# A third raw buffer and a second scaled buffer for the first block's weight tiles, in the space of the norm's tiles

## The chip, the cores and the metric

The kernel runs on one core of one Trainium2 chip. The metric is the device time of one execution in microseconds (us). TensorE (PE), VectorE (DVE), ScalarE (ACT) and GpSimd (POOL) each work through a list of instructions of their own, in order. SyncE (SP) issues all data transfers (DMAs) from one list, also in order: a transfer whose data or whose target is not ready holds back all that stand behind it.

## The reference

A linear attention with a decaying state gives 3072 rows of 384 values, and two feed-forward blocks follow.

```python
def _attn_ref(r, k, v, w, u):                 # (4, 8, 768, 48): batch, heads, steps, head size
    for t in range(S):
        kt, vt, rt, wt = (k[:, :, t], v[:, :, t], r[:, :, t], w[:, :, t])
        cur = np.einsum('bhd,bhe->bhde', u[None] * kt, vt)
        y[:, :, t] = np.einsum('bhd,bhde->bhe', rt, state + cur)
        state = wt[:, :, :, None] * state + np.einsum('bhd,bhe->bhde', kt, vt)
...
def _moe_ref(x, w_in, w_out):                 # 384 -> 2048 -> 384
    h = x @ w_in
    relu6 = np.clip(h + 3.0, 0.0, 6.0)
    g = h * relu6 / 6.0
    return g @ w_out
...
def _moe2_ref(x, w_gate, w_val, w_out, rms_g):   # 384 -> 1536 -> 384
    rms = np.sqrt(np.mean(x * x, axis=-1, keepdims=True) + 1e-06)
    xn = x / rms * rms_g
    g = xn @ w_gate
    silu = g * (1.0 / (1.0 + np.exp(-g)))
    val = xn @ w_val
    return silu * val @ w_out
```

The weights arrive as 64-bit floats, and the chip computes in 32 bits, so every weight tile is converted on the chip.

## The kernel before

**Chunks and steps.** The tokens are cut into six chunks of 512 columns (4 batches of 128 time steps). The first feed-forward block goes over the chunks c = 0 to 5 and, in each, over 16 weight tiles f = 0 to 15, one step per tile. In chunk 0, called the first block here, tiles 0 to 4 are done for the first 256 columns (steps n = 0 to 4) and then for the second 256 (n = 5 to 9), and tiles 5 to 15 for all 512 (n = 10 to 20). Chunk 1 begins at n = 21, also in half steps (n = 21 to 28 and 29 to 36). After chunk 5 follows the second feed-forward block.

A step does a first product on PE (`hps`, L353 in chunk 0, L347 later), the activation in two instructions (ACT L364, DVE L365), and the second product (`o`, L359 in chunk 0, L376 later) two steps later: `todo` holds two second products back. In chunk 0 the matmuls are plain 32-bit ones. Each `hps` has one of two PSUM buffers, which L365 frees.

**Weights.** `Weight.load` (L132) fetches a raw tile of 128 x 768 64-bit values (786 KB). `scale` (ACT, L140) brings its high words to the right exponent in a tile `mag`. `bits` (DVE, L145, L146, L148) puts the 32-bit number together in `x` from the raw tile and `mag`, and sends it to its place `wpair` by a transfer (SP, L153). `parts` (ACT L159, DVE L160) splits the tile in two for the later chunks, eleven steps after its first use (f + 11). Tile f is converted in a step n given by `begun`: f = 2 to 6 in n = 0 to 4, f = 7 and 8 in n = 7 and 8, f = 9 to 15 in n = 10 to 16. `load(f + 2)` stands in the same step right behind `bits(f)`.

**Attention.** One job per chunk and batch. The four jobs of chunk 1 (jobs 4 to 7) run beside the steps of chunk 0: job 4 begins at n = 11, job 5 at n = 15, job 6 at n = 19. From a job's step n: scans (DVE L182) and bonus (POOL L209, L210) at n; products and a sum (DVE L205, L214) at n + 1; `fill` (ACT L240, 8 instructions), `pe_a` (PE L259), `pe_kt` (PE L247) and `choose` (DVE L265, 2 instructions) at n + 2; `pe_y` (PE L295, L301), `pe_u` (PE L274), `copy_y` (ACT L307) at n + 3. `pe_y` writes the PSUM buffer that `choose` reads, and uses what `choose` wrote. For the jobs 0 to 3 of chunk 0, `pe_kt`, `copy_kt`, `pe_u` and `add_u` (ACT L281) lie in n = 2 to 6; `pe_kt` and `pe_u` share one PSUM buffer, so each `pe_kt` waits for the `add_u` before it. The loads for job 4 (`w`, `rk`, `rks`, `v`: 128 x 1040, 1024, 768 and 512 32-bit values) stand at the end of n = 7, those for job 5 (`w`, `rk`, `v`) at the end of n = 9.

**Order.** Three lists per step, `before`, `between` and `behind`, hold what runs ahead of the first product, between it and the second product, and behind it. `pin` then fixes the order of each engine as the program is written. A pool hands out buffers in rotation: a tile with `bufs=2` waits until the last reader of the tile before the previous one is done.

```python
    begun = {f: f - 2 for f in range(2, W1)} | {7: 7, 8: 8} | {f: f + 1 for f in range(9, F1)}
    for f, n in begun.items():
        before[n] += [wa[f].scale]
        behind[n] += [wa[f].bits]
        if f + 2 < F1:
            behind[n] += [wa[f + 2].load]
```

Of the kernel before, what the change touches and what calls it, by code (L numbers as in the profile page):

```python
# [9 lines left out]
F32 = mybir.dt.float32  # L10
F32R = mybir.dt.float32r
U32 = mybir.dt.uint32
U64 = mybir.dt.uint64
# [9 lines left out]
DM = H * D  # L23
KT = DM // 128
F1 = 2048 // 128
# [11 lines left out]
def kernel(  # L37
# [17 lines left out]
    def pool(stack, name, bufs=1, **kw):  # L55
        return stack.enter_context(tc.tile_pool(name=name, bufs=bufs, **kw))
# [9 lines left out]
    wp = pool(ctx, "wp", side="left")  # L66
    xt_p = pool(ctx, "xt", 2, side="left")
    rg_p = pool(ctx, "rg", 3, side="left")
    nm_p = pool(ctx, "nm", side="left")
    actx = ctx.enter_context(ExitStack())  # L70
    at_p = pool(actx, "at", 2, side="left")
    a1_p = pool(actx, "a1", side="left")
# [1 line left out]
    st_p = pool(tctx, "st", 2, side="left")  # L74
# [32 lines left out]
    def pin():  # L107
        fresh = []
        for x in reversed(nc.cur_bb.bb.instructions):
            if x.name in pinned:  # L110
                break
            fresh.append(x)
        for x in reversed(fresh):
            pinned.add(x.name)
            if x.engine in ENGINES:
                if x.engine in newest:
                    tc.add_manual_dep(x, newest[x.engine], NOSYNC, reason="program order")
                newest[x.engine] = x.name
# [2 lines left out]

    mag_bufs = 1

    class Weight:
        def __init__(self, src, dst, pairs):
            self.src, self.dst, self.pairs, self.near = src, dst, pairs, False

        def load(self):  # L130
            self.raw = st_p.tile([128, 2 * DM], U64, tag="raw", name="raw", bufs=2)
            nc.sync.dma_start(out=self.raw, in_=self.src.rearrange("p a n -> p (a n)"))  # L132

        def words(self):
# [1 line left out]
            return bits[:, :, 0], bits[:, :, 1]  # L136

        def scale(self):
            self.mag = st_p.tile([128, 2 * DM], F32, tag="mag", name="mag", bufs=mag_bufs)
            nc.scalar.activation(out=self.mag, in_=self.words()[1].bitcast(F32), func=AF.Copy, scale=2.0 ** -112)  # L140

        def bits(self):
# [288 lines left out]
    wa = [Weight(wa_d[f], None, False) for f in range(F1)]  # L431
# [8 lines left out]
    before, between, behind = ([[] for _ in steps] for _ in range(3))  # L440
# [16 lines left out]
    j0, j1, j2, j3 = jobs[:B]  # L457
# [17 lines left out]

    begun = {f: f - 2 for f in range(2, W1)} | {7: 7, 8: 8} | {f: f + 1 for f in range(9, F1)}
    for f, n in begun.items():
        before[n] += [wa[f].scale]
        behind[n] += [wa[f].bits]
        if f + 2 < F1:  # L480
            behind[n] += [wa[f + 2].load]
    for f in range(F1):
        before[f + 11] += [wa[f].parts]
    behind[7] += [lambda: jobs[4].load("w", "rk", "rks", "v")]
# [14 lines left out]
    def ff1(c, f, cols):  # L499
        n = cols.stop - cols.start  # L500
        ps = ps_h.tile([128, n], F32, tag="h", name="hps")
        if c == 0:
            if cols.start:
                wa[f].x = wpair[f][:, :, 1, :].bitcast(F32)
            emit_h_f32(wa[f].x[:, 0], xts[c][:, :, :, cols], ps)
            g = rg_p.tile([128, n], F32, tag="g", name="g")
            emit_act(ps, n, g)
        else:
            emit_h(wpair[f][:, 0], xts[c][:, :, :, cols], ps)
            a = rg_p.tile([128, n], F32, tag="a", name="a", bufs=2)  # L510
            emit_act(ps, n, a)
            g = emit_split(a, n)
        x = wa[f].x[:, 1] if c == 0 else wpair[f][:, 1]
        todo.append(lambda: ff2(c, f, cols, g, x))
# [13 lines left out]
    def run(fs):  # L528
        for x in fs:
            x()  # L530

    def load_x(c):
        x = xt_p.tile([128, KT, 2, TOK], F32R, tag="xt", name="xt")
        raw = b_p.tile([128, KT, TOK], F32, tag="xraw", name="xraw", bufs=1)
        nc.sync.dma_start(out=raw, in_=xn_d[c])
        xns[c] = x

        def part(k):
            nc.scalar.activation(out=x[:, k, 0, :], in_=raw[:, k, :], func=AF.Copy)
            nc.vector.tensor_tensor(  # L540
                out=x[:, k, 1, :], in0=raw[:, k, :], in1=x[:, k, 0, :].bitcast(F32), op=ALU.subtract)
        return part
# [22 lines left out]
    nc.sync.dma_start(out=ub, in_=u_d.to_broadcast([128, DM]))  # L565
    nc.sync.dma_start(out=gain, in_=g_d)
    wa[2].load()
    wa[3].load()
    nc.vector.memset(dd, 0.0)
    nc.vector.memset(half, 0.5)  # L570
    nc.vector.memset(eps, 1e-6)
# [4 lines left out]
        wa[f].dst = wpair[f]  # L576
        wa[f].near = f < 2
    run((j0.scans, j0.pairs, j0.pe_bonus, j0.muls, j0.fill, j0.pe_a, j1.scans, j1.pairs, j1.pe_bonus, j1.muls))
    run((j0.choose, j1.fill, j1.pe_a, j0.pe_y0, wa[0].scale, wa[0].bits, j1.choose, j1.pe_y0))
    run((j0.copy_y0, wa[1].scale, wa[1].bits, j1.copy_y0, j2.scans))  # L580
    pin()


    for n, (c, f, cols) in enumerate(steps):
        if n == W1:
            sctx.close()
            wp2 = pool(ctx, "wp2", side="right", reuse_waits="tile")
            wpair += [wp2.tile([128, 2, 2, DM], F32R, name=f"wpair{i}") for i in range(W1, F1)]
            for i in range(W1, F1):
                wa[i].dst = wpair[i]  # L590
        if n == first[1]:
            tctx.close()
        if n == first[NC_ - 1]:
            actx.close()
            st_p = pool(ctx, "st2", 2, side="left", reuse_waits="tile")
            mag_bufs = 2
            b_p = pool(ctx, "bp", 2, side="left", reuse_waits="tile")
            bw_p = pool(ctx, "bw", side="left", reuse_waits="tile")
            begun2 = {f: f * NE // F1 for f in range(F1) if (f + 1) * NE // F1 > f * NE // F1}
            extra += [bw_p.tile([128, 2, 2, DM], F32R, name=f"bpair{i}") for i in range(NX)]  # L600
            wb = [Weight(wb_d[i], extra[i] if i < NX else wpair[i - NX], True) for i in range(NB)]
            wb[0].load()
            wb[1].load()
        run(before[n])
        if c == NC_ - 1:
            if f == 4:
                part = load_x(0)
            if 8 <= f < 8 + KT:
                part(f - 8)

            if f - 2 in begun2:
                wb[begun2[f - 2]].parts()
        ff1(c, f, cols)
        run(between[n])
        while len(todo) > 2:
            todo.pop(0)()
        if c == NC_ - 1 and f in begun2:
            wb[begun2[f]].scale()
        run(behind[n])
        if c == NC_ - 1 and f in begun2:  # L620
            wb[begun2[f]].bits()
            wb[begun2[f] + 2].load()
        pin()
# [145 lines left out]
```

## Time and profile before

| | |
|---|---|
| median of 3 runs | 1025.42 us (1025.32 to 1026.27) |
| profiled execution, own time | 1027.49 us |
| its span in the trace | 1025.7 us |
| PE, DVE, ACT, POOL busy | 982.3, 484.3, 393.9, 346.4 us |
| mean granted TensorE clock | 0.987 of full |
| first step of chunk 1 (first L347) begins | 147.42 us |

Busy time is what an engine's instructions took; the span runs from the first instruction of the trace to the last. The execution's own time holds 1.8 us more than the span. The granted clock is the share of TensorE's full clock that the chip gave; it has two levels, half (1.2 GHz) and full (2.4 GHz). In the views below, a bracket at the end of a row is idle time of that engine ahead of the instruction, and what ended it.

### The profile page before, as it was taken

To read this page: it belongs to the slowest core of one execution; us is meant where nothing else is said; L and a number is where in the kernel's file an instruction comes from. 1 tells how busy PE (TensorE), PEld (TensorE's weight loads), DVE (VectorE), ACT (ScalarE), POOL (GpSimd) and SP (SyncE) were. 2 spreads that over 40 slices of the span, in tenths; PEclk is the share of its full clock that TensorE was granted. 3 is DMA by queue.
4 is the path that set the end of the run, shared out by engine and by line. 5 is a ranking of instruction groups with operands and counts; after the bars stand their busy time and mean duration, and the time that the engine had idled before them with its cause. 6 is when DMAs were issued, how large, how long until landed. Compare 5 with 4: busy or idle time off the path is not lost.

```text
span 1025.7 us, 13752 instructions
## 1 busy us (share of the span) xinstructions
PE 982.3 (96%) x5385; PEld 782.4 (76%) x5385; DVE 484.3 (47%) x627; ACT 393.9 (38%) x753; POOL 346.4 (34%) x306
## 2 busy tenths in 40 slices
PE   5797998889999999999999999999999999999998
PEld 4674457877888888787787788888888888888886
DVE  7848756665457646665389996112112112112111
ACT  3433535544544454455356554222222222222212
POOL 0002214545465574565353352222222222222221
PEclk9899989999999999999999999999999999999999
DMA  8557522333322332231242450200100100100000
GB/s 320 173 202 276 183 90 81 123 130 102 122 76 79 120 134 75 109 92 64 100 144 103 156 182 1 93 1 1 62 1 1 61 1 1 62 1 1 31 1 31
DMA packets 36768, 91.92 MB, mean 90 GB/s; under 512 B 5984, under 2 KB 17120, under 8 KB 36704
## 3 DMA queue, kind: packets, MB, share of 16 engines
q1 hardware_dynamic: 36704, 91.05, 25.6%
q8 instruction: 42, 0.69, 0.3%
q14 instruction: 22, 0.18, 0.0%
HBM read 71.37 MB, written 9.44 MB: 79 GB/s over the span
## 4 chain that ended last, share of the span: by engine, by line
PE 79%; DVE 9%; ACT 4%; DMA 4%; issue 3%; SPq 1%; POOL 0%; ACTq 0%; DVEq 0%; POOLq 0%
PE o L376 27%; PE gps L347 14%; PE vps L347 14%; PE hps L347 12%; DMA raw<-in_dram 3%; PE aps L259 2%; PE yps L301 2%; DVE x L146 2%; PE o L359 2%; PE yps L295 1%; DVE x L148 1%; PE hps L353 1%; DVE a L365 1%; PE ktp L247 1%; DVE w L182 1%
## 5 line engine op out<-in xcount | busy, mean ns | idle before, releaser
L376 PE MATMUL o<-g,wpair 128*128 128x512 f32 (+1 forms) x1287 | 306.1, 382 | 0.0
L376 PEld LDWEIGHTS o<-g,wpair 128*128 128x128 f32 x1287 | 230.4, 189 | 48.8 <-issue 0.7
L370 POOL TENSOR_TENSOR g<-s,g 128x512 fp32r<-128x512 f32 x72 | 96.8, 1344 | 338.4 <-ACT g L369 338.4
L663 DVE TENSOR_TENSOR s<-s,vps 128x512 f32<-128x512 f32 x72 | 49.5, 687 | 301.3 <-PE vps L347 300.4
L347 PE MATMUL hps<-xt,wpair 128*128 128x512 f32 (+1 forms) x792 | 182.9, 375 | 3.4 <-POOL xt L324 2.1
L370 POOL TENSOR_TENSOR g<-a,g 128x512 fp32r<-128x512 f32 (+1 forms) x88 | 113.9, 1295 | 196.7 <-ACT g L369 185.4
L347 PEld LDWEIGHTS hps<-xt,wpair 128*128 128x128 f32 x792 | 139.7, 188 | 34.2 <-POOL xt L324 2.3
L347 PE MATMUL vps<-xt,wpair 128*128 128x512 f32 x486 | 120.4, 392 | 0.0
L365 DVE SCALAR_TENSOR_TENSOR a<-a,hps 128x512 f32<-128x512 f32 (+1 forms) x88 | 55.7, 633 | 129.3 <-ACT a L364 129.2
L347 PE MATMUL gps<-xt,wpair 128*128 128x512 f32 x432 | 107.2, 392 | 0.0
L369 ACT ACTIVATE g<-s 128x512 fp32r<-128x512 f32 x72 | 45.5, 632 | 159.7 <-DVE s L663 159.7
L347 PEld LDWEIGHTS vps<-xt,wpair 128*128 128x128 f32 x486 | 91.2, 188 | 20.5
L660 ACT ACTIVATE s<-gps 128x512 f32<-128x512 f32 x72 | 43.0, 597 | 158.7 <-PE gps L347 158.7
L347 PEld LDWEIGHTS gps<-xt,wpair 128*128 128x128 f32 x432 | 81.0, 188 | 18.3
L364 ACT ACTIVATE a<-hps,half 128x512 f32<-128x512 f32 (+1 forms) x88 | 56.6, 643 | 96.1 <-PE hps L347 89.5
L369 ACT ACTIVATE g<-a 128x512 fp32r<-128x512 f32 (+1 forms) x88 | 52.2, 593 | 87.8 <-DVE a L365 86.2
L182 DVE TENSOR_TENSOR_SCAN w<-w,dd 128x520 f32<-128x520 f32 x48 | 74.8, 1559 | 4.6 <-DMA w<-in_dram 2.9
L240 ACT ACTIVATE a<-iperm,cb 128x128 f32<-128x128 f32 x192 | 58.5, 387 | 0.1
L347 PE MATMUL gps<-xt,bpair 128*128 128x512 f32 x216 | 53.0, 390 | 0.0
L209 POOL TENSOR_TENSOR rks<-rks 128x384 f32<-128x384 f32 x20 | 29.2, 1460 | 64.7 <-DMA rks<-in_dram 64.7
L347 PEld LDWEIGHTS gps<-xt,bpair 128*128 128x128 f32 x216 | 40.5, 188 | 8.8
L140 ACT ACTIVATE mag<-raw 128x768 f32<-128x768 f32 x34 | 30.6, 901 | 41.1 <-DMA raw<-in_dram 30.3
(85 smaller groups left out, 1055.8 us busy)
## 6 DMA issues: line engine op xcount, KB each, us to landing
raw<-in_dram SPq DMA_DIRECT2D x34, 768.0 KB, 4.7
w<-in_dram SPq DMA_DIRECT2D x24, 520.0 KB, 3.8
rk<-in_dram SPq DMA_DIRECT2D x24, 512.0 KB, 4.6
rks<-in_dram SPq DMA_DIRECT2D x20, 384.0 KB, 4.7
v<-in_dram SPq DMA_DIRECT2D x24, 256.0 KB, 4.8
wpair<-x SPq DMA_DIRECT2D x16, 384.0 KB, 3.2
xn<-x SPq DMA_DIRECT2D x6, 768.0 KB, 4.0
xraw<-xn SPq DMA_DIRECT2D x6, 768.0 KB, 5.0
```

Source lines behind the costliest of these rows:

```text
L140: nc.scalar.activation(out=self.mag, in_=self.words()[1].bitcast(F32), func=AF.Copy, scale=2.0 ** -112)
L182: nc.vector.tensor_tensor_scan(out=x, data0=x, data1=dd.rearrange("p a h j -> p (a h j)"), initial=0.0, op0=ALU.mult, op1=ALU.add)
L209: nc.gpsimd.tensor_tensor(out=x, in0=x, in1=self.rks[:, 1, :], op=ALU.mult)
L240: nc.scalar.activation(out=self.head(h), in_=iperm, func=AF.Copy, scale=self.cb[:, h, :])
L347: nc.tensor.matmul(ps, slot[:, l, k * 128:(k + 1) * 128], xt[:, k, r, :], start=(k == 0 and j == 0), stop=(k == KT - 1 and j == 2))
L364: nc.scalar.activation(out=a, in_=ps, func=AF.Relu, scale=1.0 / 6.0, bias=half)
L365: nc.vector.scalar_tensor_tensor(out=a, in0=a, scalar=1.0, in1=ps, op0=ALU.min, op1=ALU.mult)
L369: nc.scalar.activation(out=g[:, 0, :], in_=a, func=AF.Copy)
L370: nc.gpsimd.tensor_tensor(out=g[:, 1, :], in0=a, in1=g[:, 0, :].bitcast(F32), op=ALU.subtract)
L376: nc.tensor.matmul(acc[m][:, cols], slot[:, l, m * 128:(m + 1) * 128], g[:, r, :], start=(first and j == 0), stop=(parts or last and j == ...
L660: nc.scalar.activation(out=s, in_=gp, func=AF.Silu)
L663: nc.vector.tensor_tensor(out=s, in0=s, in1=vp, op=ALU.mult)
```

## The change

In chunk 0 the raw tiles get three buffers in place of two, and `mag` two in place of one. The space is that of the norm's tiles (`nm_p`, 14 KB in each partition), whose pool now opens at n = 21 on the other side of the memory, after the weight pool of chunk 0 is closed. `scale(f)` is written at the end of the step before (`behind[n - 1]`) and no longer at the start of its own (`before[n]`). `load(f + 3)` stands behind `bits(f)`, where `load(f + 2)` stood, and tiles 3 and 4 are loaded behind the `bits` of tiles 0 and 1.

```diff
@@ -66,7 +66,6 @@
     rg_p = pool(ctx, "rg", 3, side="left")
-    nm_p = pool(ctx, "nm", side="left")
...
@@ -121,14 +120,12 @@
-    mag_bufs = 1
...
         def load(self):
-            self.raw = st_p.tile([128, 2 * DM], U64, tag="raw", name="raw", bufs=2)
+            self.raw = st_p.tile([128, 2 * DM], U64, tag="raw", name="raw", bufs=2 if self.pairs else 3)
...
         def scale(self):
-            self.mag = st_p.tile([128, 2 * DM], F32, tag="mag", name="mag", bufs=mag_bufs)
+            self.mag = st_p.tile([128, 2 * DM], F32, tag="mag", name="mag", bufs=2)
...
@@ -475,10 +472,10 @@
     for f, n in begun.items():
-        before[n] += [wa[f].scale]
+        (behind[n - 1] if n else before[n]).append(wa[f].scale)
         behind[n] += [wa[f].bits]
-        if f + 2 < F1:
-            behind[n] += [wa[f + 2].load]
+        if f + 3 < F1:
+            behind[n] += [wa[f + 3].load]
...
     wa[2].load()
-    wa[3].load()
...
-    run((j0.choose, j1.fill, j1.pe_a, j0.pe_y0, wa[0].scale, wa[0].bits, j1.choose, j1.pe_y0))
-    run((j0.copy_y0, wa[1].scale, wa[1].bits, j1.copy_y0, j2.scans))
+    run((j0.choose, j1.fill, j1.pe_a, j0.pe_y0, wa[0].scale, wa[0].bits, wa[3].load, j1.choose, j1.pe_y0))
+    run((j0.copy_y0, wa[1].scale, wa[1].bits, wa[4].load, j1.copy_y0, j2.scans))
...
         if n == first[1]:
             tctx.close()
+            nm_p = pool(ctx, "nm", side="right", reuse_waits="tile")
...
-            mag_bufs = 2
```

The order on PE, DVE and POOL is the same before and after. On ACT it differs at two places. The first is around `fill` of job 4 at n = 13 (`a<-iperm,cb`, L240 before and L237 now); `mag<-raw` there scales tile 12. Before, on ACT:

```order
L364 ACTIVATE g_724<-hps_720,half_100 128x512
L240 ACTIVATE a_739<-iperm_97,cb_710 128x128 x8
L140 ACTIVATE mag_748<-raw_706 128x768
L159 ACTIVATE wpair2_117<-wpair2_117 128x2x384
L364 ACTIVATE g_756<-hps_752,half_100 128x512
```

And now, on ACT at the same place:

```order
L361 ACTIVATE g_723<-hps_719,half_97 128x512
L137 ACTIVATE mag_738<-raw_678 128x768
L237 ACTIVATE a_740<-iperm_94,cb_711 128x128 x8
L156 ACTIVATE wpair2_114<-wpair2_114 128x2x384
L361 ACTIVATE g_755<-hps_751,half_97 128x512
```

The scaling of tile 12 and the eight instructions of `fill` have changed places. The second place is the same with the scaling of tile 15 and `xt` of job 4 (L323 before); elsewhere a `scale` written at the end of one step and one at the start of the next are neighbours on ACT anyway, so its list does not change.

On SP the transfers keep their order, with each raw load one place earlier. Before, on SP, from the store of tile 7 to the store of tile 10 (`raw_617`, `raw_644`, `raw_679` are tiles 9, 10, 11):

```order
L153 DMA wpair7_591<-x_612 128x2x384
L132 DMA raw_617<-in_5_dram 128x768
L177 DMA w_619<-in_0_dram 128x1040
L177 DMA rk_621<-in_1_dram 128x1024
L177 DMA rks_623<-in_3_dram 128x768
L177 DMA v_625<-in_2_dram 128x512
L153 DMA wpair8_592<-x_639 128x2x384
L132 DMA raw_644<-in_5_dram 128x768
L177 DMA w_656<-in_0_dram 128x1040
L177 DMA rk_658<-in_1_dram 128x1024
L177 DMA v_660<-in_2_dram 128x512
L153 DMA wpair9_593<-x_674 128x2x384
```

Now, on SP at the same place (`raw_616`, `raw_643`, `raw_678` are tiles 10, 11, 12):

```order
L150 DMA wpair7_592<-x_611 128x2x384
L129 DMA raw_616<-in_5_dram 128x768
L174 DMA w_620<-in_0_dram 128x1040
L174 DMA rk_622<-in_1_dram 128x1024
L174 DMA rks_624<-in_3_dram 128x768
L174 DMA v_626<-in_2_dram 128x512
L150 DMA wpair8_593<-x_638 128x2x384
L129 DMA raw_643<-in_5_dram 128x768
L174 DMA w_657<-in_0_dram 128x1040
L174 DMA rk_659<-in_1_dram 128x1024
L174 DMA v_661<-in_2_dram 128x512
L150 DMA wpair9_594<-x_673 128x2x384
```

The list reads the same, but the raw load behind the store of tile 7 is now that of tile 10 instead of tile 9, and so on to the end. In the changed kernel the raw load waits for a buffer that was freed one tile earlier.

## Rows read from the trace of the kernel before

**Rows 1.** The profile's page, first line.

```profile
span 1025.7 us, 13752 instructions
```

**Rows 2.** Busy time by stretch: length, engines, granted clock, DMA share, GB/s.

```profile
44.42:72.27 27.85, 24.82 (x194) 20.88 (x193) 14.26 (x22) 10.34 (x21) 0.00 (x0) 1.00 0.42 145
72.27:147.42 75.15, 66.62 (x269) 33.80 (x268) 53.95 (x72) 29.17 (x55) 16.01 (x17) 0.93 0.59 211
147.42:230.00 82.58, 70.53 (x667) 62.11 (x666) 50.23 (x78) 43.02 (x100) 39.07 (x46) 0.94 0.30 104
230.00:1025.70 795.70, 791.48 (x4042) 641.44 (x4040) 332.22 (x403) 292.71 (x531) 289.41 (x232) 1.00 0.19 65
```

**Rows 3.** Waits of PE from 44.42 to 147.42: total, times, longest.

```profile
PE yps L295 <- DVE a L265: 6.7, 2, 3.4
PE ktp L247 <- ACT st L281: 3.0, 3, 1.4
```

**Rows 4.** Waits of ACT from 44 to 148, the same columns.

```profile
ACT mag L140 <- DMA raw<-in_dram: 29.3, 7, 8.3
...
ACT mag L140 <- DVE x L148: 10.5, 3, 4.4
```

**Rows 5.** The chain that ended last, 60 to 135: start, length, what.

```profile
74.42 8.50 DMA raw<-in_dram
...
89.44 5.99 DMA raw<-in_dram
```

**Rows 6.** PE in order of time: start, length, instruction, idle before it.

```profile
49.97 0.66 PE L247 MATMUL ktp<-ident,rk 128*128 128x128 f32 x4 [1.38 <-ACT st L281]
...
54.98 0.66 PE L247 MATMUL ktp<-ident,rk 128*128 128x128 f32 x4 [1.16 <-ACT st L281]
...
100.30 0.67 PE L295 MATMUL yps<-rk,st 64*64 64x128 f32 x16 [3.44 <-DVE a L265]
...
106.66 2.74 PE L353 MATMUL hps<-xt,wpair 128*128 128x512 f32 x6
...
130.08 1.13 PE L295 MATMUL yps<-rk,st 64*64 64x128 f32 x16 [3.30 <-DVE a L265]
...
137.52 2.74 PE L353 MATMUL hps<-xt,wpair 128*128 128x512 f32 x6
...
154.30 0.67 PE L295 MATMUL yps<-rk,st 64*64 64x128 f32 x16
...
158.65 1.63 PE L347 MATMUL hps<-xt,wpair 128*128 128x256 f32 x9
```

**Rows 7.** ACT in order of time, the same columns.

```profile
48.05 0.90 ACT L140 ACTIVATE mag<-raw 128x768 f32<-128x768 f32 x1 [3.06 <-DVE x L148]
...
53.45 0.89 ACT L140 ACTIVATE mag<-raw 128x768 f32<-128x768 f32 x1 [1.83 <-DMA raw<-in_dram]
...
74.94 0.91 ACT L140 ACTIVATE mag<-raw 128x768 f32<-128x768 f32 x1 [3.29 <-DMA raw<-in_dram]
```

**Rows 8.** Busy time by stretch, columns as in Rows 2.

```profile
72.00:88.00 16.00, 15.02 (x43) 7.74 (x42) 11.99 (x16) 3.70 (x5) 4.61 (x5) 1.00 1.01 382
100.00:108.00 8.00, 7.70 (x58) 4.70 (x59) 6.12 (x10) 2.69 (x4) 0.00 (x0) 0.79 0.47 159
128.00:136.00 8.00, 5.92 (x51) 4.50 (x52) 5.20 (x11) 1.63 (x3) 0.00 (x0) 0.57 0.17 58
```

**Rows 9.** Busy time in two stretches that end at `pe_y`, columns as in Rows 2.

```profile
74.85:100.30 25.45, 20.22 (x69) 10.16 (x68) 19.46 (x26) 10.94 (x20) 7.19 (x7) 1.00 0.84 310
...
100.30:130.08 29.78, 26.48 (x117) 13.08 (x117) 23.00 (x31) 13.09 (x24) 6.25 (x6) 0.93 0.49 171
```

**Rows 10.** SP in order of time: start, length of the issue, what.

```profile
80.37 0.55 SPq L132 DMA_DIRECT2D raw<-in_dram  x1
```

**Rows 11.** The raw loads (L132), 60 to 130: time from issue to landing.

```profile
DMA to landing us min/median/max: 4.5/6.0/8.7
```

**Rows 12.** Groups by shape, 72.27 to 147.42: busy, mean ns of one.

```profile
L240 ACT ACTIVATE a<-iperm,cb 128x128 f32<-128x128 f32 x21 | 6.4, 387 | 0.0
```

## The prediction

> **What bounds the kernel now.** The profiled execution took 1027.49 us, of which 1025.7 are the span [rows 1]; it is 2.1 us above the median of the runs shown. What I work out are differences inside the span, and I subtract them from the median, 1025.42.
>
> First the busy time by stretch [rows 2]. From 230 us on PE is busy for 791.5 of 795.7 us, so a weight tile that comes sooner can win only ahead of that. Steps 3 to 9 of chunk 0 (44.42 to 72.27) hold 27.85 - 24.82 = 3.0 us of idle PE. Steps 10 to 20 (72.27 to 147.42) hold 75.15 - 66.62 = 8.5 us, and there the granted clock is below full. From 147.42 to 230 another 12.0 us are idle.
>
> Then what PE waits for [rows 3]: three waits of `pe_kt` for `add_u`, 3.0 us, which is all of the idle time of steps 3 to 9, and two waits of `pe_y` for `choose`, 6.7 us, most of that of steps 10 to 20. Neither names a weight tile. The cause stands one engine back: ACT sits still 29.3 us for raw loads and 10.5 us for the last instruction of `bits` (L148) [rows 4], always at the head of `scale`, and all that is queued behind it (activations, `fill`, `add_u`, `parts`) waits with it. The chain that ended last runs through those loads: 8.50 us from 74.42, 5.99 us from 89.44 [rows 5]. With two raw buffers, the load of tile f + 2 is issued only when `bits(f)` is through, so that two tiles cost one load, one `scale` and one `bits` in a row.
>
> **The change part by part.** It adds no instruction and removes none. What it moves is each raw load, one tile ahead on SP, and the two swaps on ACT.
>
> *The second mag buffer.* At 48.05 `scale(5)` had waited 3.06 us for L148 [rows 7]. It will go at once after the copy ahead of it; its tile is loaded a whole step earlier. `add_u` then runs as soon as `pe_u` is done. In the third of the three waits nothing stands in the way, and it is 3.0 - 1.38 - 1.16 = 0.5 us [rows 3, 6]; this is what is left of a `pe_kt` wait. So the first gives back 1.38 - 0.5 = 0.9. The second, where `scale(6)` waited 1.83 us for its load [rows 7], gives 1.16 - 0.5 = 0.7, by the third raw buffer. Together **1.6 us** by n = 7. From there to n = 10 PE has no gap, so nothing more comes there.
>
> *The third raw buffer, steps 10 to 20.* The whole idle time of this stretch is **8.5 us** [rows 2]. Behind its two long gaps PE runs slowly. `pe_y`, `pe_u` and a second product took 106.66 - 100.30 = 6.36 us after the first gap (3.44 us) and 137.52 - 130.08 = 7.44 after the second (3.30 us); the same four groups with no gap ahead take 158.65 - 154.30 = 4.35 [rows 6]. The granted clock was 0.79 in 100 to 108 and 0.57 in 128 to 136 [rows 8], so part of each of these stretches ran at half the clock. That is 2.0 + 3.1 = **5.1 us** that go with the gaps. The ceiling is 1.6 + 8.5 + 5.1 = 15.2 us.
>
> *What is late next.* Two things meet at `pe_y` of job 4. The first is DVE. From the end of the first product of n = 10 (74.85) to `pe_y` of job 4, PE has 20.2 us of work and DVE 19.5 [rows 9]. DVE's part begins about 0.8 us later, since ACT's L364 lies between. So DVE will be done at 20.3 and PE at 20.2: nearly level, with 0.3 us for the signal between them. In the next stretch, to `pe_y` of job 5, PE has 26.5 - 2.0 (the slow clock) = 24.5 and DVE 23.0 [rows 9]: no gap.
>
> The second is the raw tile 12, ahead of `fill` now. After the change it stands on SP where tile 11 stood, behind the loads of job 5, and that load was issued at 80.37 [rows 10]. Step 10 comes 1.6 us earlier, and its activation no longer stands behind a `scale` that had waited 3.29 us [rows 7] and ended 0.9 us after PE's product did. So tile 12 is issued at 80.4 - 1.6 - 0.8 = 78.0. The slowest raw load took 8.7 us [rows 11]; I use it, for the DMA engines were busy all of 72 to 88 (share 1.01, 382 GB/s) [rows 8] and the same bytes stand ahead. It lands at 86.7. From the landing of tile 12 to `pe_y` it took 100.30 - (89.44 + 5.99) = 4.9 us [rows 5, 6]; `fill`, now in between, adds at most 8 x 0.387 = 3.1 [rows 12]. That gives 94.7, where PE is ready at 74.85 - 1.6 + 20.2 = 93.5. A gap of 1.2 us is left.
>
> The rows say that loads run no faster than this. The Trainium skill, "DMA: Bandwidth & Descriptors", section "Specifications", gives an HBM limit of some 358 GB/s for a core. The loads from tile 10 to tile 12, with those of jobs 4 and 5, are 5.39 MB by their shapes; by that figure, as an estimate, they take 15.1 us from 68.5 on and tile 12 lands at 83.6, so that only DVE's 0.3 us would be left and the sum would be 0.9 us better. The trace agrees with it as a limit: of the 382 GB/s, four fifths by the shapes come from HBM.
>
> Bounds of the residue: 0.3 us below (DVE alone); above, a gap like the old one with its slow clock, 3.3 + 2.0 = 5.3. I take 2.0, near the 1.2 worked out, since every operation must be in time for that.
>
> *At no cost.* The raw loads of tiles 2 to 4 at the start come sooner, behind all loads of jobs 0 to 3 on SP, and DVE's list, which they feed, is unchanged there. The swap with `xt` of job 4 is hidden: `xt` is needed in chunk 1, five steps later. The norm's tiles lie where the raw tiles were; the last of those is read in n = 16, and the norm's first copy is in n = 22, six steps later, so it finds them free; if that cover were gone, the copies that free the accumulators would hold up PE one for one.
>
> *Does the gain stay?* In 147 to 230 PE waits for jobs 6, 7 and later, whose loads and steps are written relative to n; all of it moves along. At n = 21 PE, ACT and DVE were level with each other before, too.
>
> **Sum.** 15.2 - 2.0 = 13.2 us: 1025.4 - 13.2 = **1012.2 us**.
>
> **The rivals.**
>
> *Loads are the bound.* With more loads in flight in a stretch whose DMA share is already 1.01 [rows 8], tiles 11 and 12 land some 3 us later than I say; the wait goes from `scale` at one step to `scale` and `fill` at n = 13. For it: the share. Against: one raw load fewer lies in that stretch, as tile 9 is loaded near 56. Price: the residue of 5.3: 15.2 - 5.3 = 9.9, 1015.5 us.
>
> *DVE is the bound.* It has 19.5 us to PE's 20.2. If its instructions are a tenth slower, being crowded against POOL's bonus and the transfers, `choose` is 2 us late for job 4 (gap and clock 4) and 1 to 2 for job 5 (2 to 4): 15.2 - 7 = 8.2, 1017.2 us.
>
> *No change.* What chunk 0 gains is waited for again in 147 to 230, because something there does not move along with n: 12.0 us of waits stand there to take it up [rows 2]. Against: no load or transfer there is tied to anything but a step. 1025.4 us.
>
> *Slower: the swap at n = 13.* `fill`, and with it `choose` and `pe_y` of job 4, now stand behind a raw load. `pe_y` stood at 100.30; 8.4 us of gain lie behind it (3.3 + 3.1 + 2.0), and a long gap costs 2.0 of them again, so the kernel is slower from `pe_y` at 106.7 on. That needs tile 12 at 106.7 - 8.0 = 98.7, 20.7 us after its issue. At 25 us in flight: 4.3 us lost, 1029.7 us. Against: no raw load took over 8.7 [rows 11].
>
> **How the numbers follow.** Chances: forecast 0.62 (own range 1010.2 to 1014.5), loads 0.17, DVE 0.11, no change 0.05, slower 0.03; 0.02 for the unforeseen. Low end: the ceiling of 15.2 with half a microsecond on top for the third `pe_kt` wait, 1009.7. High end: past the DVE case, to 1018.5. That leaves 1 in 10 above and less than 1 in 10 below. About 0.2% (2 us) is what a measurement of this kernel tells from no change. Faster by more 0.92, within it 0.05, slower 0.03.
>
> **What would show it.** In the changed trace: `scale` waits for L148 gone, and waits for raw loads well under 10 us in all; the first L347 at about 134 us; PE without a gap over 2 us between 71 and 134, at full clock; `pe_kt` waits of 0.5 us each; idle PE in the stretch that answers to 147 to 230 still 12 us. Wrong would be: a `scale` that still waits over 3 us for tiles 11 to 13, `pe_y` of job 4 later than 97, a first L347 that is early while the 12 us have grown, or a norm copy that waits for anything but PE.

## The result and the profile after

The changed kernel takes 1013.38 us (median of 4 runs, 1011.81 to 1015.42) against 1025.85 us for the kernel before in the same comparison (4 runs, 1025.32 to 1027.56). The ratio is 0.9877, 95% interval 0.9853 to 0.9900: 12.5 us or 1.2% faster. 1012.2 was forecast, with 1009.7 to 1018.5 as the range. The profiled execution took 1011.81 us, with a span of 1010.0.

Line numbers are three lower after the change: `scale` is L137, the last instruction of `bits` L145, `fill` L237, `choose` L262, the raw load L129, the first product L350 in chunk 0 and L344 later.

Busy time by stretch of the changed kernel, cut at the first product of n = 3, of n = 10 and of n = 21 and far into chunk 1, as in [rows 2] (whose first cut lies 0.2 us ahead of the first product of n = 3, at 44.63). The columns are those of [rows 2]: length, busy time of PE, its weight loads, DVE, ACT and POOL, granted clock, DMA share, GB/s.

```profile
43.40:69.85 26.45, 24.85 (x193) 20.62 (x192) 15.31 (x24) 11.10 (x21) 0.00 (x0) 1.00 0.45 154
69.85:132.82 62.97, 61.74 (x269) 31.04 (x268) 52.77 (x70) 29.24 (x55) 18.22 (x17) 1.00 0.67 239
132.82:215.40 82.58, 70.08 (x671) 61.46 (x670) 51.97 (x79) 43.13 (x100) 40.40 (x47) 0.96 0.31 104
215.40:1010.00 794.60, 790.33 (x4037) 640.68 (x4035) 331.29 (x402) 292.65 (x531) 288.70 (x231) 1.00 0.19 65
```

Steps 10 to 20 take 62.97 us in place of 75.15. PE is idle for 1.2 us there in place of 8.5, at full clock throughout. The stretch behind holds 12.5 us of idle PE where it held 12.0: those waits moved along and took back half a microsecond at most.

What PE waits for in steps 3 to 20, and what `scale` on ACT waits for (total, times, longest):

```profile
PE ktp L244 <- ACT st L278: 1.5, 3, 0.5
PE yps L292 <- POOL rks L207: 1.1, 1, 1.1
```

```profile
ACT mag L137 <- DMA raw<-in_dram: 7.2, 2, 4.0
```

Against [rows 3] the waits of `pe_kt` fell from 3.0 to 1.5 us, those of `pe_y` from 6.7 to 1.1; against [rows 4] `scale` waits 7.2 us for raw loads in place of 29.3, and not at all for L148 (L145 now). The two waits that are left are those for tiles 11 and 12.

PE, ACT, DVE and SP of the changed kernel in order of time (start, length, instruction, idle before it), at the place of [rows 6, 7 and 10]:

```profile
47.85 0.66 PE L244 MATMUL ktp<-ident,rk 128*128 128x128 f32 x4 [0.49 <-ACT st L278]
...
93.62 0.67 PE L292 MATMUL yps<-rk,st 64*64 64x128 f32 x16 [1.11 <-POOL rks L207]
...
98.37 2.74 PE L350 MATMUL hps<-xt,wpair 128*128 128x512 f32 x6
...
118.17 0.67 PE L292 MATMUL yps<-rk,st 64*64 64x128 f32 x16
...
122.92 2.74 PE L350 MATMUL hps<-xt,wpair 128*128 128x512 f32 x6
...
132.82 1.62 PE L344 MATMUL hps<-xt,wpair 128*128 128x256 f32 x9
```

```profile
80.43 0.92 ACT L137 ACTIVATE mag<-raw 128x768 f32<-128x768 f32 x1 [3.24 <-DMA raw<-in_dram]
...
86.64 0.93 ACT L137 ACTIVATE mag<-raw 128x768 f32<-128x768 f32 x1 [3.97 <-DMA raw<-in_dram]
87.46 2.43 ACT L237 ACTIVATE a<-iperm,cb 128x128 f32<-128x128 f32 x8
```

```profile
92.13 1.34 DVE L262 COPY_PREDICATED a<-mask,aps 128x512 f32<-128x512 uint32 x2
```

```profile
77.26 0.56 SPq L129 DMA_DIRECT2D raw<-in_dram  x1
```

The raw loads of the changed kernel from 60 to 120 took, from issue to landing:

```profile
DMA to landing us min/median/max: 4.5/4.9/9.3
```

Tile 12 is issued at 77.3 (forecast 78.0), and its scaling starts at 86.6 (forecast landing 86.7); the load took 9.3 us in place of the 8.7 assumed. `fill` stands behind it, `choose` ends at 92.13 + 1.34 = 93.47, and `pe_y` of job 4 starts 0.15 us later after a gap of 1.1 us (forecast 1.2). The view puts that gap down to POOL's L207. That is the bonus of job 5, written at n = 15, a step behind this `pe_y`; the instruction that ended 0.15 us ahead and that `pe_y` needs is `choose`. The prediction allowed 0.3 us for that signal; 0.15 is what the rows show. `pe_y` of job 5 (118.17) has no gap at all.

Not all of 147.42 - 132.82 = 14.6 us is the change's. The first matmul of the execution began at 9.27 us before and at 8.08 after, behind the first loads and the first work on them, which the change doesn't touch:

```profile
8.08 1.86 PE L225 MATMUL cps<-uc,rp 128*128 128x2 f32 x8 [8.08 <-DVE rp L219]
```

In the traces of all kernels of this study it begins between 8.07 and 9.60 us. The times that were forecast are counted from the start of the trace of before; counted from the first matmul, 1.2 us earlier here, tile 12 is issued 0.5 us and landed 1.1 us later than forecast, and `pe_y` of job 4 (94.7 forecast) comes 0.1 us later. From the first matmul to the first product of chunk 1 it took 138.2 us before and 124.7 after: 13.4 less, 1.2 of them in steps 3 to 9 and 12.2 in steps 10 to 20. The kernels are compared below by the time from the start of the third waiting `pe_kt` (n = 6) to the first product of chunk 1, in one trace each, beside their times.

### The profile page after: what moved, and what is told of

Same layout as the page of the kernel before. It is cut to its first block, busy times and chain, and to the rows that moved or that the text cites. A ratio compares the mean times of both kernels' runs of the same rounds, so it can differ in the third digit from the quotient of the medians.

```text
span 1010.0 us, 13759 instructions
## 1 busy us (share of the span) xinstructions
PE 976.5 (97%) x5385; PEld 778.5 (77%) x5385; DVE 485.2 (48%) x627; ACT 394.9 (39%) x753; POOL 349.2 (35%) x306
## 3 DMA queue, kind: packets, MB, share of 16 engines
q1 hardware_dynamic: 36704, 91.05, 25.8%
## 4 chain that ended last, share of the span: by engine, by line
PE 84%; DVE 6%; ACT 3%; DMA 2%; issue 2%; SPq 1%; POOL 1%; ACTq 0%; DVEq 0%; POOLq 0%
PE o L373 27%; PE gps L344 15%; PE vps L344 15%; PE hps L344 12%; PE hps L350 3%; PE o L356 3%; PE aps L256 2%; PE yps L298 2%; PE yps L292 1%; DVE a L362 1%; PE ktp L244 1%; PE yps L333 1%; DVE x L143 1%; PE ups L271 1%; DMA x<-y 1%
## 5 line engine op out<-in xcount | busy, mean ns | idle before, releaser
L344 PE MATMUL hps<-xt,wpair 128*128 128x512 f32 (+1 forms) x792 | 183.5, 376 | 3.7 <-POOL xt L321 2.0
L344 PEld LDWEIGHTS hps<-xt,wpair 128*128 128x128 f32 x792 | 140.3, 189 | 34.4 <-POOL xt L321 2.2
L344 PE MATMUL vps<-xt,wpair 128*128 128x512 f32 x486 | 120.4, 392 | 0.0
L344 PE MATMUL gps<-xt,wpair 128*128 128x512 f32 x432 | 107.1, 392 | 0.0
L344 PEld LDWEIGHTS vps<-xt,wpair 128*128 128x128 f32 x486 | 91.2, 188 | 20.4
L344 PEld LDWEIGHTS gps<-xt,wpair 128*128 128x128 f32 x432 | 81.0, 188 | 18.2
L237 ACT ACTIVATE a<-iperm,cb 128x128 f32<-128x128 f32 x192 | 58.5, 387 | 2.7 <-DVE cb L211 2.6
L344 PE MATMUL gps<-xt,bpair 128*128 128x512 f32 x216 | 53.0, 390 | 0.0
L344 PEld LDWEIGHTS gps<-xt,bpair 128*128 128x128 f32 x216 | 40.5, 188 | 8.8
L145 DVE SCALAR_TENSOR_TENSOR x<-mag,x 128x768 uint32<-128x768 uint32 x34 | 43.7, 1284 | 4.4 <-ACT mag L137 2.0
```

The lines of the kernel that those rows point to most:

```text
L145: nc.vector.scalar_tensor_tensor(out=x, in0=self.mag.bitcast(U32), scalar=3, in1=x, op0=ALU.logical_shift_left, op1=ALU.bitwise_or)
L237: nc.scalar.activation(out=self.head(h), in_=iperm, func=AF.Copy, scale=self.cb[:, h, :])
L344: nc.tensor.matmul(ps, slot[:, l, k * 128:(k + 1) * 128], xt[:, k, r, :], start=(k == 0 and j == 0), stop=(k == KT - 1 and j == 2))
```

## The experiments

All ratios are to the kernel before, run on the same chip. "Stretch" is the time just described.

| kernel | ratio (95% interval) | stretch, us |
|---|---|---|
| before | 1 | 59.32 to 147.42: 88.1 |
| norm's pool moved alone | 1.0011 (0.9997 to 1.0025) | 58.55 to 144.39: 85.8 |
| two raw, two mag buffers | 1.0021 (1.0003 to 1.0039) | 59.26 to 146.71: 87.5 |
| three raw, two mag, loads two ahead | 1.0007 (0.9990 to 1.0025) | 59.04 to 144.73: 85.7 |
| three raw, one mag | 0.9961 (0.9946 to 0.9977) | 57.73 to 139.58: 81.9 |
| four raw, one mag | 0.9936 (0.9918 to 0.9955) | 58.50 to 139.35: 80.9 |
| the change, tile 12 late | 0.9945 (0.9925 to 0.9965) | 57.49 to 140.11: 82.6 |
| the change | 0.9877 (0.9853 to 0.9900) | 56.90 to 132.82: 75.9 |
| the change, again | 0.9897 (0.9874 to 0.9920) | 57.80 to 133.49: 75.7 |
| the change, `scale` at its own step | 0.9885 (0.9869 to 0.9902) | 58.84 to 134.17: 75.3 |
| the change, job 5 loaded later | 0.9896 (0.9873 to 0.9918) | 57.30 to 132.40: 75.1 |
| both of the last two | 0.9876 (0.9860 to 0.9892) | 57.74 to 133.07: 75.3 |
| both, again | 0.9895 (0.9873 to 0.9916) | 55.80 to 131.21: 75.4 |

**The norm's pool moved alone.**

```diff
 # to the kernel before
-    nm_p = pool(ctx, "nm", side="left")
...
             tctx.close()
+            nm_p = pool(ctx, "nm", side="right", reuse_waits="tile")
```

> The kernel before, with the norm's pool opened at n = 21 on the other side of the memory as in the change; raw tiles keep two buffers, mag one, loads and scale stay where they were. Theory (the gain comes from the weight tiles alone): no change, 1024.5 to 1026.5 us, norm copies wait for PE only. Rival (the new place of the norm's and the attention's tiles matters by itself): off by 1 us or more.

1026.06 us, ratio 1.0011: no gain. The interval reaches from 0.3 us faster to 2.6 us slower, so a loss of the 1 us that the rival names is not excluded; the gain of the change can't come from here. The stretch is 85.8 us in this trace and 88.1 in that of the kernel before, with the same work and the same two gaps of 3.44 and 3.30 us at `pe_y`: some 2 us of what one trace shows of this stretch are its own. The first gap shows one source of that:

```profile
99.10 0.67 PE L294 MATMUL yps<-rk,st 64*64 64x128 f32 x16 [3.44 <-DVE a L264]
...
103.85 2.74 PE L352 MATMUL hps<-xt,wpair 128*128 128x512 f32 x6
```

The four groups behind it take 4.75 us here, at a granted clock of 1.00, where they took 6.36 behind the same gap in [rows 6].

**Two raw and two mag buffers.**

```diff
 # to the change
-            ... name="raw", bufs=2 if self.pairs else 3)
+            ... name="raw", bufs=2)
...
-        if f + 3 < F1:
-            behind[n] += [wa[f + 3].load]
+        if f + 2 < F1:
+            behind[n] += [wa[f + 2].load]
```

Tile 3 is loaded ahead of the steps again and tile 4 where it was.

> The change with two raw buffers again and load(f + 2) where it was before; the second mag buffer, the place of scale and the norm's new place stay. Theory (late raw loads are what holds ACT): the waits of scale for L148 go, those for raw loads stay near 29 us or grow, the first pe_kt wait falls to 0.5 us and the second stays near 1.2, pe_y of jobs 4 and 5 still wait some 3 us each; 1021 to 1025 us. Rival (the single mag buffer was what mattered): 1016 us or less.

1026.14 us, ratio 1.0021 (1021 to 1025 were expected): nothing gained, perhaps a little lost. The waits of ACT, by the same view as [rows 4], and the two `pe_kt` of [rows 6]:

```profile
ACT mag L137 <- DMA raw<-in_dram: 33.8, 8, 7.8
```

```profile
48.81 0.66 PE L244 MATMUL ktp<-ident,rk 128*128 128x128 f32 x4 [0.49 <-ACT st L278]
...
54.92 0.66 PE L244 MATMUL ktp<-ident,rk 128*128 128x128 f32 x4 [1.88 <-ACT st L278]
```

The 10.5 us for L148 are gone, and the wait for loads has grown by 4.5 us. The first `pe_kt` gains its 0.9 us; the second, behind a load that still is as late, loses 0.7 of them.

**Three raw buffers, one mag buffer.**

```diff
 # to the change
-            ... name="mag", bufs=2)
+            ... name="mag", bufs=2 if self.pairs else 1)
```

> The change with one mag buffer again; three raw buffers, early loads and the place of scale stay. By the prediction's account the mag buffer is worth 0.9 us, so 1014 us. Rival: with one buffer, scale of tile f + 1 at the end of a step stands in wait for bits(f), and the next activation behind it, so that a step costs L364, L365, bits, scale and parts in a row, some 5.4 us, and more where fill, scans or products lie between; then PE waits again at n = 12 to 16 and the time is 1018 to 1021 us, with over 10 us of waits of scale for L148 and hardly any for raw loads.

1019.35 us, ratio 0.9961: four of the twelve microseconds. The rival was right, the prediction's account was not. The waits of `scale` on ACT, and ACT, DVE and PE around tiles 11 and 12:

```profile
ACT mag L137 <- DVE x L145: 18.0, 6, 5.6
...
ACT mag L137 <- issue: 12.1, 3, 4.5
...
ACT mag L137 <- DVE dd L184: 3.3, 1, 3.3
```

```profile
85.26 0.93 ACT L137 ACTIVATE mag<-raw 128x768 f32<-128x768 f32 x1 [5.62 <-DVE x L145]
...
91.05 0.90 ACT L137 ACTIVATE mag<-raw 128x768 f32<-128x768 f32 x1 [3.56 <-DVE x L145]
91.86 2.43 ACT L237 ACTIVATE a<-iperm,cb 128x128 f32<-128x128 f32 x8
```

```profile
84.22 0.96 DVE L145 SCALAR_TENSOR_TENSOR x<-mag,x 128x768 uint32<-128x768 uint32 x1
...
90.01 0.96 DVE L145 SCALAR_TENSOR_TENSOR x<-mag,x 128x768 uint32<-128x768 uint32 x1
```

```profile
98.00 1.13 PE L292 MATMUL yps<-rk,st 64*64 64x128 f32 x16 [4.66 <-DVE a L262]
```

`scale` waits 33 us again, where it had waited 40, but now for DVE: that of tile 11 begins at 85.26, when `bits` of tile 10 has ended (84.22 + 0.96), that of tile 12 at 91.05, when `bits` of tile 11 has (90.01 + 0.96), and `fill`, `parts` and the next activation stand behind. The 12.1 us under "issue", for which the view names nothing, end in the same way: at 100.36 the last instruction of `bits` had just ended (99.32 + 0.96). One gap of 4.7 us at `pe_y` of job 4 is left, the one at job 5 is gone. In this kernel `fill` stands behind the scaling of tile 12, as in the change; one mag buffer with `scale` at the start of its own step was not run, so how much of the gap is the buffer's alone, and how much the place of `scale` adds to it, is not shown.

**Four raw buffers, one mag buffer.**

```diff
 # to three raw, one mag
-            ... name="raw", bufs=2 if self.pairs else 3)
+            ... name="raw", bufs=2 if self.pairs else 4)
...
-        if f + 3 < F1:
-            behind[n] += [wa[f + 3].load]
+        if f + 4 < F1:
+            behind[n] += [wa[f + 4].load]
```

Tiles 3 to 5 are loaded one place earlier to match.

> Four raw buffers, loads four tiles ahead, one mag buffer. If the single mag buffer is what is left over in the run with three raw buffers and one mag buffer, it is the same again: waits of scale for L148, one long gap at pe_y of job 4, 1017 to 1021 us. If depth of loading mattered: 1014 us or less.

1018.6 us, ratio 0.9936. The gap at `pe_y` of job 4, and two of the three rows of waits of `scale`:

```profile
98.74 1.13 PE L292 MATMUL yps<-rk,st 64*64 64x128 f32 x16 [4.65 <-DVE a L262]
```

```profile
ACT mag L137 <- issue: 21.3, 5, 5.6
ACT mag L137 <- DVE x L145: 8.8, 4, 3.1
```

`scale` waits 33 us in all, and no row names a load: deeper loading doesn't replace the mag buffer.

**Three raw buffers, loads at their old place.**

```diff
 # to the change
-        if f + 3 < F1:
-            behind[n] += [wa[f + 3].load]
+        if f + 2 < F1:
+            behind[n] += [wa[f + 2].load]
```

Tile 3 is loaded ahead of the steps again and tile 4 where it was; the buffers stay three and two.

> The change with three raw and two mag buffers, but each raw load at its old place, two tiles ahead. Theory (a load waits on SP behind the store of the tile before it, so the place in the list decides and a free buffer alone starts no load earlier): as with two raw and two mag buffers, 1023 to 1026 us, waits of scale for raw loads some 34 us. Rival (the buffer alone helps): 1018 us or less.

1025.08 us, ratio 1.0007, as expected, with both gaps at `pe_y` there (4.30 and 3.13 us):

```profile
ACT mag L137 <- DMA raw<-in_dram: 33.7, 8, 7.8
```

A free buffer starts no load: the load's place on SP does, behind the store of a tile that isn't ready.

**Scale at its own step.**

```diff
 # to the change
-        (behind[n - 1] if n else before[n]).append(wa[f].scale)
+        before[n] += [wa[f].scale]
```

> The change with scale written at the start of its own step again, as before, so that fill of job 4 stands ahead of the scaling of tile 12 on ACT (and xt of job 4 ahead of that of tile 15); the rest of ACT's list is the same. Theory (the buffers make the gain, the place of scale in the code nothing): all but the gap at pe_y of job 4 stays; fill starts at the sum's end near 86.1 instead of 87.5, tile 12 is scaled behind it, and parts and choose come some 0.5 us sooner, so that the gap falls from 1.1 to about 0.6 us; the time does not change measurably. Rival (scaling a step ahead is what wins): several us slower than the change.

1013.76 us, ratio 0.9885: as the change. ACT and PE at n = 13 and 14:

```profile
87.97 2.45 ACT L237 ACTIVATE a<-iperm,cb 128x128 f32<-128x128 f32 x8 [3.28 <-DVE cb L211]
90.33 0.90 ACT L137 ACTIVATE mag<-raw 128x768 f32<-128x768 f32 x1
```

```profile
94.97 0.67 PE L292 MATMUL yps<-rk,st 64*64 64x128 f32 x16 [0.53 <-POOL rks L207]
```

With `fill` ahead of the scaling of tile 12 again, the gap is 0.53 us in place of 1.1 (0.6 was expected). The scaling "a step ahead" wins nothing here; the swap it brings costs about half a microsecond (the gap is 0.89 us in a second trace of the change).

**Job 5 loaded later.**

```diff
 # to the change
-    behind[9] += [lambda: jobs[5].load("w", "rk", "v")]
+    behind[10] += [lambda: jobs[5].load("w", "rk", "v")]
```

> The change with the loads of job 5 one step later, behind the raw load of tile 12 instead of ahead of it. Theory (the 1.1 us that are left at pe_y of job 4 come from tile 12's late landing ahead of fill): scale of tile 12 waits under 1.5 us instead of 4.0, the gap at pe_y of job 4 falls to 0.3 us or less, 0.8 us less in all, too little for the timing to tell surely; scans of job 5 at n = 15 do not wait. Rival (DVE is what is late at choose): the gap stays at 1 us.

1012.49 us, ratio 0.9896. ACT and PE at the same place:

```profile
84.82 0.92 ACT L137 ACTIVATE mag<-raw 128x768 f32<-128x768 f32 x1 [1.72 <-DVE x L145]
```

```profile
93.20 0.67 PE L292 MATMUL yps<-rk,st 64*64 64x128 f32 x16 [0.30 <-DVE a L262]
```

With 1.3 MB of loads taken from ahead of tile 12, its scaling waits for a mag buffer and no longer for the load (1.7 us; under 1.5 was expected), and 0.30 us of the gap are left, as the prediction had it for DVE. DVE has no idle time from 81.6 to the end of `choose` in this trace. So 0.6 to 0.8 us of the gap were the late tile. The time can't tell it from the change.

**Both moves together,** that is the edits of the last two kernels.

> The change with the loads of job 5 one step later and scale at the start of its own step. The gap at pe_y of job 4 is 0.3 us, DVE's part, as with the later loads alone, since choose then waits for DVE; no measurable difference to the change, 1011 to 1014 us, perhaps 0.8 us less.

> The change with the loads of job 5 one step later and scale at the start of its own step, beside the change on one chip: from the first matmul to the first product of chunk 1 0.5 to 0.8 us less, in the time no difference that can be told.

1012.78 us (ratio 0.9876), and 1013.16 (0.9895) beside the change's 0.9897 on one chip. The gap at `pe_y` of job 4 is 0.5 us in both traces; 0.3 was expected, and what the rest waits for is not shown. From the first matmul to the first product of chunk 1 it takes 124.2 and 122.7 us, against 124.7 and 125.4 for the change: some of it by chance, and nothing that the time shows.

**Tile 12 late.**

```diff
 # to the change
-        if f + 3 < F1:
+        if f == 10:
+            behind[n] += [wa[12].load]
+        if f + 3 < F1 and f != 9:
             behind[n] += [wa[f + 3].load]
```

> The change with one raw load moved: that of tile 12 stands behind bits of tile 10 instead of tile 9, so it is issued some 8 us later. It tests the price in the prediction: tile 12 then lands near 90 instead of 86.6, fill, choose and pe_y of job 4 come some 3.4 us later, the gap at pe_y grows from 1.1 to 4.5, and the products behind it run at half the clock for a while, about 2 us more: 5 us slower than the change, some 1018 us. Rival (the lateness is taken up before the end): within 2 us of the change.

1019.29 us, ratio 0.9945, 5 to 7 us slower than the change by the ratios. ACT at n = 13, and PE:

```profile
91.81 0.90 ACT L137 ACTIVATE mag<-raw 128x768 f32<-128x768 f32 x1 [8.53 <-DMA raw<-in_dram]
```

```profile
98.76 1.13 PE L292 MATMUL yps<-rk,st 64*64 64x128 f32 x16 [5.68 <-DVE a L262]
...
105.66 2.74 PE L350 MATMUL hps<-xt,wpair 128*128 128x512 f32 x6
```

Counted from the third `pe_kt`, tile 12 is scaled 4.6 us later than in the change (91.81 - 57.49 against 86.64 - 56.90), not 3.4; it is issued in one go with tile 13, and both are in flight together. The gap grows by as much, and the four groups behind it take 105.66 - 98.76 = 6.9 us in place of 4.75: 2.15 us for the clock. Together that is 6.7 us, just what the stretch grew by (82.6 against 75.9): a late tile at n = 13 is paid in full.

**The change again.**

> The change once more, for the spread of its times and a second trace: ratio to the kernel before 0.986 to 0.990. From the first matmul to the first product of chunk 1 it takes 124.7 us within 0.5, as in the first trace; what differs between runs is the start (first matmul at 8.0 to 9.6 us) and which of the gaps between 155 and 215 us are followed by half the clock.

1014.13 us, ratio 0.9897. The stretch is 75.7 us (75.9 in the first trace), and the gap at `pe_y` of job 4 is 0.89. From the first matmul it took 125.4 us in place of 124.7, a little more than the 0.5 allowed; the difference lies ahead of n = 3.

## Why the prediction was right, point by point

**What bounds the kernel.** Right. Weight tiles are nowhere named in PE's waits, and held up ACT; with the waits at the head of `scale` down from 40 to 7 us, PE's waits at `pe_kt` and `pe_y` went with them. The experiments carry it both ways: leave either wait in place and `scale` waits 33 to 34 us again.

**The second mag buffer: 0.9 us.** This step failed. As the prediction put it, the mag buffer frees one `pe_kt` and the whole gain of steps 10 to 20 is the third raw buffer's. By itself the mag buffer gives nothing (ratio 1.0021), and on top of three raw buffers it takes the stretch from 81.9 to 75.9 us, the time from 0.9961 to 0.9877 (0.9897 the second time), with `scale` written a step ahead in both. The two waits stood in parallel at one instruction, and the view puts each wait down to the later of the two; take one away, and 33 to 34 of the 40 us come back under the other's name. The prediction read 29.3 and 10.5 us as shares, and they are not. As the change does both, the sum didn't suffer; that was luck, not reckoning.

**The third raw buffer, 8.5 us of idle PE.** PE's idle time in steps 10 to 20 fell to 1.2 us, so 7.3 came back. It takes the earlier place of the loads on SP besides the buffers: with three and two buffers and the loads at their old place nothing is gained (ratio 1.0007).

**The clock, 5.1 us.** That slow stretches went with the gaps was right for the trace that was read; the term is 0.8 too large for it, and larger than the gaps cost in the other traces. The four groups behind `pe_y` take 98.37 - 93.62 = 4.75 and 122.92 - 118.17 = 4.75 us at full clock, not 4.35; so (6.36 - 4.75) + (7.44 - 4.75) = 4.3. The reference, 154.30 to 158.65, was followed by a product of half the width, which starts 2.28 us after the start of the product ahead of it, in place of 2.68. And the gaps don't set the size of the loss. Reckoned in the same way against 4.75 us, the three other kernels that keep both gaps lose 1.6 us (norm's pool moved alone), 1.5 (loads two ahead) and 3.2 (two raw, two mag) behind gaps of 3.1 to 4.4 us. The trace of before had the largest loss of the four, so the term was a draw of that trace: with 1.5 to 3.2 in place of 5.1 the sum would have been 9.6 to 11.3 us, not 13.2.

**The residue, 2.0 us.** 1.2 was derived, 1.1 measured (0.89 in the second trace), and in part by luck, as its parts erred both ways: the load came 1.1 us later than worked out, and from there to `pe_y` it took 93.62 - 86.64 = 7.0 us for at most 8.0, in part because the eight instructions of `fill` overlap (2.43 us for 3.1). The 0.8 on top were caution. That it was the load and not DVE, and that DVE stood 0.3 us behind it, the later loads of job 5 show. The rival "loads are the bound" has the right place and is paid as it said when the load is late (6.7 us of stretch for 4.6); it didn't come about because the load took 9.3 us and not 12.

**The estimate from the HBM limit.** By the figure of the Trainium skill, "DMA: Bandwidth & Descriptors", "Specifications" (358 GB/s from HBM), tile 12 could have landed at 83.6, as an estimate. The trace does not bear that landing out: counted from the first matmul it came 4 us later. The backlog moved at the rate of the row, 367 GB/s with the stores of the tiles in it, the engines at a share of 1.01:

```profile
68.00:88.00 20.00, 19.88 (x74) 11.27 (x73) 16.43 (x23) 7.80 (x12) 5.46 (x5) 1.00 1.01 367
58.20:59.60 1.40, 1.40 (x9) 1.22 (x8) 0.00 (x0) 0.06 (x1) 0.00 (x0) 1.00 0.98 404
```

Nor does it bear the figure out as a limit at every moment: in the second row only packets of one raw load are moved, at 404 GB/s for 1.4 us.

**The first 1.6 us.** The waits of `pe_kt` fell by 1.5. The stretch from n = 3 to n = 10 shortened by 27.64 - 26.45 = 1.2 (hps at 44.63 to 72.27 before, 43.40 to 69.85 after).

**The size.** 13.2 forecast; 12.5 measured, and 10.5 by the ratio on another chip (0.9897). The stretch was 88.1 us in the one trace of before, and 85.7 to 87.5 in three kernels that wait the same way, so that trace was a long one, mostly by its clock, and a ceiling drawn from it was up to two microseconds high. That the sum came so near is in part luck. "No change", "slower" and "DVE" did not come about.

**The signs of being wrong.** One of them came true: `scale` still waits over 3 us for two of the tiles 11 to 13 (3.24 us for tile 11, 3.97 for tile 12). The sign was ill chosen, as the sum itself let tile 12 land late, at 86.7. No view shows a wait of PE from 69.85 to `pe_y` of job 4, so the two waits cost it no more than the 1.1 us there. Another came true by name only: for one of the three norm copies in chunk 1 (L389) the view names a transfer in place of PE, but the wait is 1.48 us, as long as with the norm's pool moved alone, where the name is PE. The norm's tiles found their space free.

## What to carry to other kernels

Where an instruction waits for two things, a view shows the later one only; read the waits as a maximum, and ask of each what remains when it alone is taken away. The Trainium skill, "Trainium Kernel Development and Optimization", "Best Practices", advises double buffers. Here two raw and two scaled ones gave nothing (ratio 1.0021), and three and two gave 1.0 to 1.2%. Our reading, not tested beyond these kernels, is that the depth that is needed follows from how many steps lie between the load's place in its queue and its use. A buffer more was worth nothing here (1.0007) until the load was also written earlier in the in-order list that issues it. And take a gap's price at the clock from more than one trace.

## What the hardware showed unexpectedly

The clock behind a gap is not set by the gap's length. The gap of 4.38 us at `pe_y` of job 7 was followed by half the clock in the first trace of the change and by the full one in the second, in two executions of one kernel. First trace, then second:

```profile
158.19 1.13 PE L292 MATMUL yps<-rk,st 64*64 64x128 f32 x16 [4.38 <-POOL g L367]
```

```profile
158.86 0.67 PE L292 MATMUL yps<-rk,st 64*64 64x128 f32 x16 [4.38 <-POOL g L367]
```

So 2 us for the clock behind a gap is what it may cost, not what it must. What decides it is not shown. The kernel before varied from 1020.4 to 1027.4 us over 17 runs on one chip, and the clock goes with it: the mean granted clock was 0.989 to 0.990 in the four fastest of them and 0.983 to 0.987 in the six slowest.
